# A mixture-of-experts kernel: weights loaded and split in 1024-column pieces, VectorE's lower halves a call behind

## The chip, the cores and the metric

The kernel runs on one core of one Trainium2 chip. The metric is the time of one execution in device microseconds; the text compares medians of several runs. TensorE (PE in the rows) multiplies, VectorE (DVE), ScalarE (ACT) and GpSimd (POOL) do the elementwise work, and SyncE (SP) issues most of the DMAs.

## What is computed

```python
def reference(...):
    # 1: gated linear attention, 4 x 8 heads, 768 steps, head size 48
    state = alpha[t][:, None] * state + outer(k[t], v[t]);  y[t] = q[t] @ state
    x = y, reshaped to 3072 rows of 384
    # 2: first mixture: rows whose skip score is over 0 go to one of 8 experts (384 -> 1024 -> 384)
    e = argmax(x @ w_gate);  x += gate * (relu(x @ w1[e]) @ w2[e])
    # 3: second mixture: all rows, the same sizes, weights of its own, without the residual
    e = argmax(x @ w_gate2); out = gate * (relu(x @ w1b[e]) @ w2b[e])
```

Inputs and outputs are float32. An expert's products are done in three 16-bit matmuls: each operand is split into an upper half (float16) and a lower half (the rest), and upper x upper, upper x lower and lower x upper are summed.

## The kernel before

The kernel has three stages. Attention runs over 24 groups of 128 steps (g = 0 to 23); for each group VectorE makes two scans (`pp`, L546, and `qka`, L550), GpSimd or VectorE multiply them into k and q (L554, L555), TensorE forms the products (`ap`, `kp`, `yp`, `sp`, `rp`), ScalarE evicts, and one of the two masks is on GpSimd (`at`, L572) and the other on VectorE (L574). The first mixture runs over nine rounds (j = 0 to 8) of up to 256 rows, rounds 0 and 1 with the same expert; the second mixture has nine rounds of up to 480 rows. In a round `ffn1` makes the hidden layer in pairs of 128 columns (first mixture): TensorE writes `hp`, ScalarE evicts the upper half `hh`, VectorE the lower half `hl`. `ffn2t` then makes `yp`, evicted as `yth` and `ytl`. Beside that, a generator `gate_rows` of the round before works out on VectorE where each row goes next: among its steps are `own`, `mv` and `hot` (the one-hot tile, L372), which TensorE multiplies into an index, `idx_ps` (L377). From the index GpSimd issues indirect DMAs that gather the rows (`xg`).

The order of the instructions is written out by hand: `tick`, `tick2` and the like are called after each piece of matmul work, and step the generators (`rt`, `release`) and the weight work (`background`) by tables of numbers.

Weights: `load_w(x, m)` loads matrix m (0 for w1, 384 x 1024, and 1 for w2, 1024 x 384) of expert x, 16 experts counting both mixtures, in one DMA on SyncE's queue into a float32 tile `raw` of 3072 columns; there are two such places. `queue_split` puts four pieces of 768 columns on a list, and each call of `background` takes one: ScalarE copies it to the upper half (`w0h` for w1, `w1h` for w2, L202), and VectorE or GpSimd subtract to give the lower half (`w0l`, `w1l`, L207). `ON_POOL` names the pieces whose subtraction is GpSimd's: 0 and 2 of expert 0, 1 to 3 of experts 1 to 8, none after that. The first GpSimd piece behind a VectorE piece is one column wider, so that it waits for it.

In attention `background` is called at even g from 6 on; in rounds 2 to 8 of the first mixture at f = 1, 3, 5, 7 of `ffn1` and four times in `ffn2t`.

Of the kernel before, what the change touches and what calls it, by code (L numbers as in the profile page):

```python
# [8 lines left out]
F32 = mybir.dt.float32  # L9
# [3 lines left out]
AF = mybir.ActivationFunctionType  # L13
ALU = mybir.AluOpType
# [59 lines left out]
ON_POOL = [(0, 2)] + [(1, 2, 3)] * 8 + [()] * 7  # L74
# [34 lines left out]
def body(tc, qka, vN, rw, wg2, wg17, w1a, w2a, w1b, w2b, cst, zr, out):  # L109
    nc = tc.nc  # L110
    V, A, P, T, SY = nc.vector, nc.scalar, nc.gpsimd, nc.tensor, nc.sync
    ctx = ExitStack()
    with ctx:
# [20 lines left out]

        with ExitStack() as fctx, tc.manual_schedule():
            wsp = fctx.enter_context(tc.tile_pool(name="wsp", bufs=2))
            wraw = fctx.enter_context(tc.tile_pool(name="wraw", bufs=2))
            em = fctx.enter_context(tc.tile_pool(name="em", bufs=1))
            ps = fctx.enter_context(tc.tile_pool(name="ps", bufs=1, space=PSUM))

# [3 lines left out]
            def bank(tag, name, *shape, parts=128):  # L144

                pool, bufs = phase.get(tag, (ps, 1))
                t = pool.tile([128, 512], F32, tag=tag, name=name, bufs=bufs)
                v = t[0:parts, 0:int(np.prod(shape))]
                if len(shape) == 2:
                    v = v.rearrange("p (a b) -> p a b", a=shape[0])  # L150
                elif len(shape) == 3:
                    v = v.rearrange("p (a b c) -> p a b c", a=shape[0], b=shape[1])
                return v
# [28 lines left out]
            raw = {}  # L182
            wt = {}
            regs = {}

            def load_w(x, m):
                if x >= 2 * E:
                    return
                src = ((w1a, w2a), (w1b, w2b))[x // E][m]
                src = src[bass.ds(regs[x], 1)].rearrange("o k f -> (o k) f") if x % E else src[0]  # L190
                t = wraw.tile([128, 3072], F32, tag="raw", name=f"raw{x}_{m}")
                kc = 3 if m == 0 else 8
                SY.dma_start(t.rearrange("p (k f) -> p k f", k=kc), src.rearrange("(k p) f -> p k f", p=128))
                raw[x, m] = t

            def split_w(x, m, s):
                if s == 0:
                    wt[x, m] = [wsp.tile([128, 3072], d, tag=f"w{m}{h}", name=f"w{m}{h}_{x}") for h, d in (("h", F16), ("l", BF16))]
                hi, lo = wt[x, m]
                r = raw[x, m]  # L200
                sl = slice(s * 768, (s + 1) * 768)
                A.activation(out=hi[:, sl], in_=r[:, sl], func=AF.Copy)  # L202
                eng = P if s in ON_POOL[x] else V
                if x and s and eng is P and s - 1 not in ON_POOL[x]:

                    sl = slice(s * 768 - 1, (s + 1) * 768)
                eng.tensor_tensor(lo[:, sl], r[:, sl], hi[:, sl], op=ALU.subtract)  # L207

            bg = []

            def queue_split(x, m):
                if x < 2 * E:
                    for s in range(4):
                        bg.append((x, m, s))

            def background(n=1):
                for _ in range(n):
                    if bg:
                        split_w(*bg.pop(0))

# [169 lines left out]
            def order(i, counts):  # L392
# [27 lines left out]
                for s in range(1, 8):  # L420
                    regs[8 * i + s] = nc.values_load(
                        perm[:, i, s:s + 1], engines=[mybir.EngineType.SP], min_val=0, max_val=7,
                        skip_runtime_bounds_check_because="places of a permutation of the experts")
                load_w(8 * i + 1, 0)
                yield 0
                cap = cc("caps")[:, 8 * i:8 * i + 8].rearrange("p (s o) -> p s o", o=1).to_broadcast([128, 8, 8])
# [26 lines left out]

            def ffn1(x, n, nf, xs, hs, each):

                (xh, xl), (hh, hl) = xs, hs
                wh, wl = [w.rearrange("p (k f) -> p k f", k=3) for w in wt[x, 0]]
                for f0 in range(0, 8, nf):
                    hp = bank("B", "hp", nf, n)
                    for i in range(nf):  # L460
                        f = slice((f0 + i) * 128, (f0 + i + 1) * 128)
                        for k in range(3):
                            T.matmul(hp[:, i], lhsT=wh[:, k, f], rhs=xh[:, k, 0:n], start=(k == 0), stop=False)  # L463
                            T.matmul(hp[:, i], lhsT=wh[:, k, f], rhs=xl[:, k, 0:n], start=False, stop=False)  # L464
                            T.matmul(hp[:, i], lhsT=wl[:, k, f], rhs=xh[:, k, 0:n], start=False, stop=(k == 2))  # L465
                        if i < nf - 1:
                            each(f0 + i)
                    A.activation(out=hh[:, f0:f0 + nf, 0:n], in_=hp, func=AF.Relu)  # L468
                    V.scalar_tensor_tensor(out=hl[:, f0:f0 + nf, 0:n], in0=hp, scalar=0.0, in1=hh[:, f0:f0 + nf, 0:n], op0=ALU.max, op1=ALU.subtract)  # L469
                    each(f0 + nf - 1)  # L470

            def ffn2(x, yp, hs, c, each):

                wh, wl = [w.rearrange("p (f d) -> p f d", f=8) for w in wt[x, 1]]
                for f in range(8):
                    T.matmul(yp, lhsT=hs[0][:, f, c], rhs=wh[:, f], start=(f == 0), stop=False)
                    T.matmul(yp, lhsT=hs[0][:, f, c], rhs=wl[:, f], start=False, stop=False)
                    T.matmul(yp, lhsT=hs[1][:, f, c], rhs=wh[:, f], start=False, stop=(f == 7))
                    each(f)

            def ffn2t(x, c0, c1, hs, yps, each):

                wh, wl = [w.rearrange("p (f d) -> p f d", f=8) for w in wt[x, 1]]
                for d, yp in enumerate(yps):
                    ds = slice(d * 128, (d + 1) * 128)
                    for f in range(8):
                        T.matmul(yp, lhsT=wh[:, f, ds], rhs=hs[0][:, f, c0:c1], start=(f == 0), stop=False)  # L487
                        T.matmul(yp, lhsT=wh[:, f, ds], rhs=hs[1][:, f, c0:c1], start=False, stop=False)  # L488
                        T.matmul(yp, lhsT=wl[:, f, ds], rhs=hs[0][:, f, c0:c1], start=False, stop=(f == 7))  # L489
                        each(d, f)  # L490
# [252 lines left out]
            emit_a(0)  # L743
            prep(2, halves)
            queue_split(0, 0)
            queue_split(0, 1)
            routes, orders = [], []
            for g in range(NB):
# [5 lines left out]
                if g > 0:  # L754
                    emit_r(g - 1)
                    i, k, n, _ = gof[g - 1]
# [30 lines left out]
                if g in (3, 6):  # L787
                    load_w(0, g // 6)
# [132 lines left out]
            for j in range(NJ):  # L921
                x = POS[j]
# [4 lines left out]
                if j != 1:  # L927
                    queue_split(x + 1, 0)
# [71 lines left out]
            for j in range(NJ):  # L1000
                x = E + POS[j]
# [84 lines left out]
                if j == 0:  # L1086

                    tot = bank("M", "tot", 18)
                    for c, src in ((0, cum[:, len(GROUPS), 0:8]), (8, cum2[:, NJ, :]), (16, cum[:, SPLIT, 0:1]), (17, cum2[:, NJ - LAST, 0:1])):
                        w = src.shape[-1]  # L1090
# [139 lines left out]
```

## Time and profile before

| | us |
|---|---|
| median of 3 runs | 529.93 (529.77 to 530.51) |
| the profiled execution | 529.54 |
| its span in the trace | 527.70 |
| TensorE busy | 491.6 (93%) |
| VectorE busy | 363.2 (69%) |
| GpSimd busy | 274.7 (52%) |
| ScalarE busy | 270.2 (51%) |

The times in the rows are microseconds from the start of the span. A row of the timeline gives start, duration, engine, line, operation and what is written from what, how many such instructions are merged, and in brackets how long the engine had been idle before and what ended that. TensorE's busy time is a share of the span by modelled ends of its matmuls; where it waits, a bracket says so.

### The profile page before, as it was taken

How to read it: one execution, taken by the hardware profiler on the slowest of the kernel's cores; microseconds unless marked ns; L12 is line 12 of the kernel's file. 1: busy time of each engine (PE TensorE's matmuls, PEld its weight loads, DVE VectorE, ACT ScalarE, POOL GpSimd, SP SyncE). 2: the span in 40 equal slices, each digit the busy share in tenths (PEclk: the TensorE clock that was granted, in tenths of full speed). 3: DMA queues.
4: the chain of work that ended last, by engine and by line, in shares of the span. 5: the costliest groups of instructions: out<-in, count | busy, mean ns of one | idle time of the engine just before them, and what ended most of it. 6: DMA issues, size and time to landing. Idle time of an engine off the chain costs nothing.

```text
span 527.7 us, 12035 instructions
## 1 busy us (share of the span) xinstructions
PE 491.6 (93%) x4701; PEld 378.5 (72%) x4701; DVE 363.2 (69%) x927; ACT 270.2 (51%) x545; POOL 274.7 (52%) x226
## 2 busy tenths in 40 slices
PE   5899998999986999998989899999999999999992
PEld 3788887878885999898979566565555666666662
DVE  7989997989697677888778845845537373737320
ACT  1545555465543666656656244734556464646320
POOL 2479978698426867687866153227024151311121
PEclk9999999999999999999999999999999999999997
DMA  8889784771285657767774076583535445450010
GB/s 282 324 293 324 221 278 152 254 226 48 64 255 185 204 172 259 254 202 267 223 260 145 25 252 245 161 281 89 176 111 188 149 154 169 139 186 29 17 39 27
DMA packets 44868, 96.74 MB, mean 183 GB/s; under 512 B 7049, under 2 KB 31879, under 8 KB 44806
## 3 DMA queue, kind: packets, MB, share of 16 engines
q1 hardware_dynamic: 36614, 77.68, 44.5%
q0 software_dynamic: 4736, 13.51, 7.6%
q10 hardware_dynamic: 3456, 4.72, 2.5%
q8 instruction: 39, 0.64, 0.5%
q14 instruction: 23, 0.19, 0.1%
HBM read 83.41 MB, written 12.99 MB: 183 GB/s over the span
## 4 chain that ended last, share of the span: by engine, by line
PE 59%; DVE 23%; issue 6%; POOL 5%; DMA 4%; ACT 1%; POOLq 0%; ACTq 0%; DVEq 0%
PE hp L463 8%; PE hp L465 8%; PE hp L464 8%; PE ypc L487 4%; PE ypc L489 4%; PE ypc L488 4%; DVE pp L546 4%; DVE qka L550 4%; PE tp L450 3%; PE yp L488 2%; PE yp L489 2%; PE yp L487 2%; DMA xg<-xrows,ixb 2%; PE rp L645 2%; DMA raw<-in_w1a 2%
## 5 line engine op out<-in xcount | busy, mean ns | idle before, releaser
L982 POOL DMA_INDIRECT out<-o,ixo x31 | 31.4, 1011 | 142.0 <-ACT o L1055 127.2
L469 DVE SCALAR_TENSOR_TENSOR h2l<-hp,h2h 128x352 f16<-128x352 f32 (+8 forms) x66 | 38.6, 585 | 64.1 <-ACT h2h L468 63.1
L463 PE MATMUL hp<-x2h,w0h 128*128 128x352 f16 (+8 forms) x216 | 68.7, 323 | 0.0
L465 PE MATMUL hp<-x2h,w0l 128*128 128x352 f16 (+8 forms) x216 | 68.7, 323 | 0.0
L464 PE MATMUL hp<-x2l,w0h 128*128 128x352 f16 (+8 forms) x216 | 68.7, 323 | 0.0
L468 ACT ACTIVATE h2h<-hp 128x352 f16<-128x352 f32 (+8 forms) x66 | 33.8, 513 | 46.6 <-PE hp L465 46.5
L207 POOL TENSOR_TENSOR w1l<-raw,w1h 128x768 bf16<-128x768 f32 (+1 forms) x26 | 43.0, 1681 | 27.0 <-ACT w1h L202 16.6
L463 PE MATMUL hp<-xh,w0h 128*128 128x200 f16 (+7 forms) x216 | 52.4, 252 | 4.8 <-DVE hl L469 3.9
L202 ACT ACTIVATE w0h<-raw 128x768 f16<-128x768 f32 x64 | 53.4, 836 | 4.5 <-ACT xy L646 1.7
L464 PEld LDWEIGHTS <-w0h 128*128 128x128 f16 x432 | 42.3, 98 | 18.5 <-issue 5.2
L441 POOL DMA_INDIRECT xg<-xrows,ix x41 | 49.2, 1200 | 11.6 <-issue 9.3
L488 PE MATMUL yp<-hl,w1h 128*128 128x200 f16 (+7 forms) x216 | 53.4, 255 | 0.5 <-DVE hl L469 0.4
L202 ACT ACTIVATE w1h<-raw 128x768 f16<-128x768 f32 x64 | 51.5, 836 | 4.3 <-DMA raw<-in_w2a 2.2
L487 PE MATMUL yp<-hh,w1h 128*128 128x200 f16 (+7 forms) x216 | 53.5, 255 | 0.0
L489 PE MATMUL yp<-hh,w1l 128*128 128x200 f16 (+7 forms) x216 | 53.5, 255 | 0.0
L465 PEld LDWEIGHTS <-w0l 128*128 128x128 bf16 x432 | 42.3, 98 | 15.2 <-issue 0.4
L464 PE MATMUL hp<-xl,w0h 128*128 128x200 f16 (+7 forms) x216 | 52.3, 252 | 0.1
L465 PE MATMUL hp<-xh,w0l 128*128 128x200 f16 (+7 forms) x216 | 52.4, 252 | 0.0
L463 PEld LDWEIGHTS <-w0h 128*128 128x128 f16 x432 | 42.3, 98 | 13.6 <-issue 0.5
L207 DVE TENSOR_TENSOR w0l<-raw,w0h 128x768 bf16<-128x768 f32 x38 | 39.7, 1046 | 13.0 <-ACT w0h L202 10.9
L207 POOL TENSOR_TENSOR w0l<-raw,w0h 128x768 bf16<-128x768 f32 (+1 forms) x26 | 44.1, 1720 | 4.7 <-ACT w0h L202 2.4
L554 POOL TENSOR_TENSOR qka<-qka 128x512 f32<-128x512 f32 (+1 forms) x24 | 28.5, 1186 | 29.8 <-DVE qka L550 22.9
(183 smaller groups left out, 1350.5 us busy)
## 6 DMA issues: line engine op xcount, KB each, us to landing
qka<-in_qka SPq DMA_DIRECT2D x21, 772.0 KB, 6.9
raw<-in_w1a SPq DMA_DIRECT2D x8, 1536.0 KB, 6.8
raw<-in_w2a SPq DMA_DIRECT2D x8, 1536.0 KB, 8.9
raw<-in_w1b SPq DMA_DIRECT2D x8, 1536.0 KB, 7.3
raw<-in_w2b SPq DMA_DIRECT2D x8, 1536.0 KB, 7.1
v<-in_vN SPq DMA_DIRECT2D x24, 192.0 KB, 3.5
xrows<-xy ACTq DMA_DIRECT2D x24, 192.0 KB, 4.4
xrows<-x SPq DMA_DIRECT2D x9, 197.0 KB, 4.8
```

The source lines that it names most:

```text
L202: A.activation(out=hi[:, sl], in_=r[:, sl], func=AF.Copy)
L207: eng.tensor_tensor(lo[:, sl], r[:, sl], hi[:, sl], op=ALU.subtract)
L441: P.indirect_dma_start(out=dst, out_offset=None, in_=xrows[0:rows], in_offset=bass.IndirectOffsetOnAxis(ap=ix, axis=0), bounds_check=rows ...
L463: T.matmul(hp[:, i], lhsT=wh[:, k, f], rhs=xh[:, k, 0:n], start=(k == 0), stop=False)
L464: T.matmul(hp[:, i], lhsT=wh[:, k, f], rhs=xl[:, k, 0:n], start=False, stop=False)
L465: T.matmul(hp[:, i], lhsT=wl[:, k, f], rhs=xh[:, k, 0:n], start=False, stop=(k == 2))
L468: A.activation(out=hh[:, f0:f0 + nf, 0:n], in_=hp, func=AF.Relu)
L469: V.scalar_tensor_tensor(out=hl[:, f0:f0 + nf, 0:n], in0=hp, scalar=0.0, in1=hh[:, f0:f0 + nf, 0:n], op0=ALU.max, op1=ALU.subtract)
L487: T.matmul(yp, lhsT=wh[:, f, ds], rhs=hs[0][:, f, c0:c1], start=(f == 0), stop=False)
L488: T.matmul(yp, lhsT=wh[:, f, ds], rhs=hs[1][:, f, c0:c1], start=False, stop=False)
L489: T.matmul(yp, lhsT=wl[:, f, ds], rhs=hs[0][:, f, c0:c1], start=False, stop=(f == 7))
L982: ins = P.indirect_dma_start(out=out, out_offset=bass.IndirectOffsetOnAxis(ap=ix, axis=0), in_=src, in_offset=None, bounds_check=N - 1, oo ...
```

## The change

There are six places of 1024 columns in place of two of 3072, the same memory. A w1 matrix is loaded and split in three pieces of 1024 columns, a w2 matrix in four of 768; each piece has a DMA and a place of its own, and a piece's load waits only for the piece six before it. ScalarE's upper half is issued by the call of `background` that takes the piece. If the lower half is VectorE's, it goes on a list `lows` and is issued by the next call, before that call's own piece; if it is GpSimd's, it is issued at once. The one column by which GpSimd's first piece was wider becomes an instruction of its own, since it lies in another place. `split_done` makes sure that a matrix is complete before its matmuls.

```diff
-            wraw = fctx.enter_context(tc.tile_pool(name="wraw", bufs=2))
+            wraw = fctx.enter_context(tc.tile_pool(name="wraw", bufs=6))
...
+            PIECES = ([(i * 1024, (i + 1) * 1024) for i in range(3)], [(i * 768, (i + 1) * 768) for i in range(4)])
             def load_w(x, m):
...
-                t = wraw.tile([128, 3072], F32, tag="raw", name=f"raw{x}_{m}")
-                kc = 3 if m == 0 else 8
-                SY.dma_start(t.rearrange("p (k f) -> p k f", k=kc), src.rearrange("(k p) f -> p k f", p=128))
-                raw[x, m] = t
+                src = src.rearrange("(k p) f -> p k f", p=128)
+                w = src.shape[2]
+                for s, (a, b) in enumerate(PIECES[m]):
+                    t = raw[x, m, s] = wraw.tile([128, 1024], F32, tag="raw", name=f"raw{x}_{m}{s}")
+                    SY.dma_start(t[:, 0:b - a].rearrange("p (k f) -> p k f", f=w), src[:, a // w:b // w, :])
+            lows = []
             def split_w(x, m, s):
...
-                A.activation(out=hi[:, sl], in_=r[:, sl], func=AF.Copy)
-                eng = P if s in ON_POOL[x] else V
-                if x and s and eng is P and s - 1 not in ON_POOL[x]:
-
-                    sl = slice(s * 768 - 1, (s + 1) * 768)
-                eng.tensor_tensor(lo[:, sl], r[:, sl], hi[:, sl], op=ALU.subtract)
+                A.activation(out=hi[:, a:b], in_=r[:, 0:b - a], func=AF.Copy)
+                if s not in ON_POOL[x]:
+                    lows.append((x, m, s))
+                    return
+                if x and s and s - 1 not in ON_POOL[x]:
+
+                    a0, b0 = PIECES[m][s - 1]
+                    P.tensor_tensor(lo[:, b0 - 1:b0], raw[x, m, s - 1][:, b0 - a0 - 1:b0 - a0], hi[:, b0 - 1:b0], op=ALU.subtract)
+                P.tensor_tensor(lo[:, a:b], r[:, 0:b - a], hi[:, a:b], op=ALU.subtract)
+            def flush():
+                for x, m, s in lows:
+                    hi, lo = wt[x, m]
+                    a, b = PIECES[m][s]
+                    V.tensor_tensor(lo[:, a:b], raw[x, m, s][:, 0:b - a], hi[:, a:b], op=ALU.subtract)
+                lows.clear()
...
             def background(n=1):
                 for _ in range(n):
+                    flush()
                     if bg:
                         split_w(*bg.pop(0))
+            def split_done(x, m):
+
+                while any(b[0:2] == (x, m) for b in bg):
+                    background()
+                if any(b[0:2] == (x, m) for b in lows):
+                    flush()
```

VectorE's queue at the start of round 4, before (names as above; a number behind a name is its buffer, and line numbers are each program's own):

```order
L353 TENSOR_REDUCE own<-ge 128x2
L469 SCALAR_TENSOR_TENSOR hl<-hp,hh 128x2x232
L207 TENSOR_TENSOR w0l_3262<-raw_0_3091,w0h_3261 128x768
L356 TENSOR_TENSOR own<-cs,own 128x16
L469 SCALAR_TENSOR_TENSOR hl<-hp,hh 128x2x232
L360 SCALAR_TENSOR_TENSOR own<-own,r 128x2
L365 TENSOR_TENSOR mv<-on,own 128x128
```

The same place of VectorE's queue in the changed program:

```order
L378 TENSOR_REDUCE own<-ge 128x2
L495 SCALAR_TENSOR_TENSOR hl<-hp,hh 128x2x232
L381 TENSOR_TENSOR own<-cs,own 128x16
L495 SCALAR_TENSOR_TENSOR hl<-hp,hh 128x2x232
L223 TENSOR_TENSOR w0l_3310<-raw_00_3128,w0h_3309 128x1024
L385 SCALAR_TENSOR_TENSOR own<-own,r 128x2
L390 TENSOR_TENSOR mv<-on,own 128x128
```

The lower half w0l moves behind the second pair's hl and is 1024 columns wide.

VectorE's queue at the end of round 0, where the index read (ixr, ixb) releases a gather, before:

```order
L939 TENSOR_SCALAR gs<-xg 128x2
L940 TENSOR_SCALAR gs<-xg 128x2
L207 TENSOR_TENSOR w0l_2317<-raw_0_2073,w0h_2316 128x768
L387 COPY ixr<-idx_ps 128x48
L388 SCALAR_TENSOR_TENSOR own<-idx_ps,ixr 128x48
L702 CAST ixb<-own 128x1
```

The same place in the changed program, down to where w0l now stands:

```order
L967 TENSOR_SCALAR gs<-xg 128x2
L968 TENSOR_SCALAR gs<-xg 128x2
L412 COPY ixr<-idx_ps 128x48
L413 SCALAR_TENSOR_TENSOR own<-idx_ps,ixr 128x48
L730 CAST ixb<-own 128x1
L732 TENSOR_TENSOR own<-idx_94,own 128x48
L459 TENSOR_TENSOR pr<-place_95,own 128x98
L462 TENSOR_REDUCE own<-pr 128x14
L463 CAST ix_114<-own 128x14
L735 COPY idx_94<-own 128x32
L976 TENSOR_TENSOR ytl_2194<-yp,yth_2193 128x200
L223 TENSOR_TENSOR w0l_2335<-raw_00_2081,w0h_2334 128x1024
```

The lower half goes from ahead of the index read to behind the first ytl.

GpSimd's queue in attention, from its second lower half of w1 (w0l, at g = 10) on, before:

```order
L207 TENSOR_TENSOR w0l_706<-raw_0_504,w0h_705 128x768
L572 AFFINE_SELECT at<-at 128x512
L554 TENSOR_TENSOR qka<-qka 128x512
L555 TENSOR_TENSOR qka<-qka,pp 128x512
L572 AFFINE_SELECT at<-at 128x512
L554 TENSOR_TENSOR qka<-qka 128x512
L555 TENSOR_TENSOR qka<-qka,pp 128x512
L572 AFFINE_SELECT at<-at 128x512
```

The same stretch of the changed program's queue, from its second w0l on:

```order
L217 TENSOR_TENSOR w0l_716<-raw_02_508,w0h_715 128x1024
L600 AFFINE_SELECT at<-at 128x512
L582 TENSOR_TENSOR qka<-qka 128x512
L583 TENSOR_TENSOR qka<-qka,pp 128x512
L600 AFFINE_SELECT at<-at 128x512
L582 TENSOR_TENSOR qka<-qka 128x512
L583 TENSOR_TENSOR qka<-qka,pp 128x512
L217 TENSOR_TENSOR w1l_1198<-raw_10_707,w1h_1197 128x768
L600 AFFINE_SELECT at<-at 128x512
```

The first w2 piece (w1l) of expert 0 comes on GpSimd 6 rows of `qka` and `at` work behind that w0l; before it came after 12, two groups later. The third w2 piece moves by two groups as well.

## Rows read from the trace of the kernel before

**Rows 1.** Busy time by stage: stretch, length, engines (instructions), TensorE's granted clock, DMA share, GB/s.
```profile
146.00:174.00 28.00, 22.26 (x323) 21.31 (x323) 22.18 (x86) 11.56 (x26) 13.94 (x16) 0.94 0.66 215
...
170.00:171.00 1.00, 1.00 (x12) 0.94 (x11) 0.93 (x8) 0.31 (x2) 0.00 (x0) 0.50 1.02 420
...
174.00:291.00 117.00, 110.56 (x1183) 105.72 (x1180) 92.64 (x316) 73.13 (x130) 86.05 (x63) 1.00 0.67 221
...
318.00:508.00 190.00, 190.00 (x1174) 114.85 (x1173) 100.83 (x192) 99.34 (x175) 54.50 (x49) 1.00 0.43 144
```

**Rows 2.** TensorE's longest wait: us in total, times, longest.
```profile
PE idx_ps L377 <- DVE hot L372: 7.1, 5, 2.6
```

**Rows 3.** Timeline of round 4, several engines.
```profile
206.31 4.85 POOL L207 TENSOR_TENSOR w1l<-raw,w1h 128x769 bf16<-128x769 f32 x3 [3.79 <-DVE w1l L207]
...
210.42 1.55 DVE L207 TENSOR_TENSOR w0l<-raw,w0h 128x768 bf16<-128x768 f32 x1
...
210.88 0.56 ACT L468 ACTIVATE hh<-hp 128x464 f16<-128x464 f32 x1 [0.50 <-PE hp L465]
...
212.52 0.15 DVE L360 SCALAR_TENSOR_TENSOR own<-own,r 128x2 f32<-128x2 f32 x1
...
216.01 0.23 PE L377 MATMUL idx_ps<-mv,hot 128*128 128x64 f16 x2 [0.92 <-DVE hot L372]
```

**Rows 4.** Timeline of rounds 6, 7 and 8, several engines.
```profile
239.66 4.86 POOL L207 TENSOR_TENSOR w1l<-raw,w1h 128x769 bf16<-128x769 f32 x3 [3.96 <-DVE w1l L207]
...
256.90 0.13 POOL L942 MEMSET x<- 128x16 f32 x1
256.98 4.85 POOL L207 TENSOR_TENSOR w1l<-raw,w1h 128x769 bf16<-128x769 f32 x3
...
260.57 0.84 ACT L202 ACTIVATE w0h<-raw 128x768 f16<-128x768 f32 x1 [1.54 <-DMA raw<-in_w1a]
...
266.60 0.23 PE L377 MATMUL idx_ps<-mv,hot 128*128 128x64 f16 x2 [2.64 <-DVE hot L372]
...
283.33 0.25 PE L488 MATMUL yp<-hl,w1h 128*128 128x200 f16 x1 [0.36 <-DVE hl L469]
```

**Rows 5.** Timeline of rounds 0 and 1, several engines.
```profile
155.57 0.95 DVE L207 TENSOR_TENSOR w0l<-raw,w0h 128x768 bf16<-128x768 f32 x1
...
161.00 4.83 POOL L207 TENSOR_TENSOR w0l<-raw,w0h 128x769 bf16<-128x769 f32 x3
...
161.70 0.26 PE L450 MATMUL tp<-cs,xg 80*128 80x80 f32 x1 [1.43 <-DMA xg<-xrows,ixb]
...
162.87 3.01 DVE L969 COPY cum<-cum 128x8 f16<-128x8 f16 x1
...
168.03 0.20 PE L463 MATMUL hp<-xh,w0h 128*128 128x80 f16 x1 [2.97 <-DVE hl L469]
```

**Rows 6.** Timeline of attention, several engines.
```profile
49.33 0.44 SPq L531 DMA_DIRECT2D qka<-in_qka  x1
...
55.15 2.58 POOL L207 TENSOR_TENSOR w0l<-raw,w0h 128x768 bf16<-128x768 f32 x1
...
77.56 2.58 POOL L207 TENSOR_TENSOR w0l<-raw,w0h 128x768 bf16<-128x768 f32 x1
...
81.72 0.31 PE L606 MATMUL yp<-at,v 128*48 128x128 f32 x1 [1.61 <-POOL at L572]
...
86.14 1.29 DVE L207 TENSOR_TENSOR w0l<-raw,w0h 128x768 bf16<-128x768 f32 x1 [0.33 <-ACT w0h L202]
...
114.22 1.19 POOL L554 TENSOR_TENSOR qka<-qka 128x512 f32<-128x512 f32 x1 [1.18 <-DVE qka L550]
...
117.53 0.38 PE L566 MATMUL ap<-qka 64*128 64x128 f32 x2 [1.10 <-POOL qka L555]
```

**Rows 7.** DMA issues: what, queue, times, KB each, median us from issue to landing.
```profile
raw<-in_w1a SPq DMA_DIRECT2D x8, 1536.0 KB, 6.8
...
v<-in_vN SPq DMA_DIRECT2D x24, 192.0 KB, 3.5
```

More of the change, by code (lines that the diff above doesn't have):

```diff
@@ L199, in split_w @@
                 hi, lo = wt[x, m]
-                r = raw[x, m]
-                sl = slice(s * 768, (s + 1) * 768)
-                A.activation(out=hi[:, sl], in_=r[:, sl], func=AF.Copy)
-                eng = P if s in ON_POOL[x] else V
-                if x and s and eng is P and s - 1 not in ON_POOL[x]:
-                    sl = slice(s * 768 - 1, (s + 1) * 768)
-                eng.tensor_tensor(lo[:, sl], r[:, sl], hi[:, sl], op=ALU.subtract)
+                r = raw[x, m, s]
+                a, b = PIECES[m][s]
[10 more added lines that the diff above has]
+                    hi, lo = wt[x, m]
+                    a, b = PIECES[m][s]
+                    V.tensor_tensor(lo[:, a:b], raw[x, m, s][:, 0:b - a], hi[:, a:b], op=ALU.subtract)
+                lows.clear()
             bg = []
@@ L212, in queue_split @@
                 if x < 2 * E:
-                    for s in range(4):
+                    for s in range(len(PIECES[m])):
                         bg.append((x, m, s))
@@ L454, in ffn1 @@
             def ffn1(x, n, nf, xs, hs, each):
+                split_done(x, 0)
                 (xh, xl), (hh, hl) = xs, hs
@@ L472, in ffn2 @@
             def ffn2(x, yp, hs, c, each):
+                split_done(x, 1)
                 wh, wl = [w.rearrange("p (f d) -> p f d", f=8) for w in wt[x, 1]]
@@ L481, in ffn2t @@
             def ffn2t(x, c0, c1, hs, yps, each):
+                split_done(x, 1)
                 wh, wl = [w.rearrange("p (f d) -> p f d", f=8) for w in wt[x, 1]]
```

## The prediction, made before the changed kernel was run

> **What bounds the kernel now.** I read the busy time and granted clock by stage first, then who TensorE waits for, then the order of time around each of those waits. By stage [rows 1], TensorE is busy for all 190 us of the second mixture's steady part (318 to 508), 110.56 of 117 us in rounds 2 to 8 of the first mixture (174 to 291) and 22.26 of 28 us in rounds 0 and 1. So a weight load or split that moves in the second mixture costs nothing as long as the weights are ready, and what the change is worth is read from the idle TensorE time of attention and of the first mixture. The list of TensorE's waits has one large entry, the index matmul for VectorE's one-hot tile "hot": 7.1 us in five places [rows 2]. Four of these are in rounds 4 to 7, once a round, such as 0.92 us at 216.01 [rows 3] and 2.64 us at 266.60 [rows 4]. The others are in rounds 0 and 1 [rows 5] and in attention [rows 6].
>
> **What sets those waits.** In rounds 4 to 7 VectorE works without a pause from the first pair's lower half to "hot". One row on the way is too long: w0l takes 1.55 us from 210.42 [rows 3], where the same instruction takes 0.95 at 155.57 [rows 5]. GpSimd's three w1l pieces end at 206.31 + 4.85 = 211.16, and w0l ends 0.81 later, at 211.97 [rows 3]. VectorE was held until GpSimd's run ended. Round 7 looks like a late load, as ScalarE waits 1.54 us for raw, but GpSimd's w1l run ends only at 256.98 + 4.85 = 261.83 [rows 4], so w0l, which follows that ScalarE piece, would have been held anyway. The copy of cum at 162.87 tells more: it arrives in the second of three w0l pieces on GpSimd and ends at 165.88, right after the third (161.00 + 4.83 = 165.83) [rows 5]. GpSimd does not let VectorE in between pieces queued back to back.
>
> The Trainium skill ("SBUF — State Buffer", section "SBUF: two separate sides") says that VectorE with two SBUF inputs, or in a fast mode, and GpSimd lock each other out of a shared port for a whole instruction. By that rule alone the copy would have got in after the second piece, 1.6 us earlier; the measured row decides. With the rule, round 6 below would gain 0.2 us and rounds 0 and 1 would give less, and the sum would be about +1.6 instead of +1.45.
>
> **The change part by part.** A w1 piece grows by a third in width, so by at most a third in time: VectorE's 0.95 becomes at most 1.27 (I take 1.2, as a part of it is fixed), GpSimd's 1.62 (a third of 4.85) at most 2.16. A w2 piece keeps its width. The one-column GpSimd instruction is not in the trace; it lies between GpSimd's memset of 16 columns, 0.13 us [rows 4], and 1.62; I take 0.2, by the memset.
>
> *Rounds 4 and 5.* The flush puts w0l behind the second pair's lower half hl. Before, w0l filled the time in which VectorE waits for that pair: hl could only start when ScalarE's hh of 210.88 ended, near 211.44 [rows 3]. Afterwards VectorE idles until 211.44, hl runs for 0.55 (211.97 to 212.52 before, from w0l's end to the next row), w0l for 1.2, and the next instruction (own, L360) starts near 213.2 instead of 212.52 [rows 3]. Everything from there to "hot" is the same chain, so the wait at 216.01 grows by 0.65. Round 5 has the same pattern: +1.3 for both. GpSimd's run starts later too, since VectorE's w1l now stands behind a ytl (some 0.7 us), ends near 212.0 and just misses holding w0l.
>
> *Round 6.* GpSimd's run ends at 239.66 + 4.86 = 244.52 [rows 4], plus up to 0.9 for the later w1l and the one-column piece. w0l, by the pattern of round 4 ready at about that time, is free or held 0.5 us: +0.1 to +0.55; I take +0.3.
>
> *Round 7.* ScalarE's late load goes away, as the first piece needs only its own place. w0l is still held to 261.83 or a little later, so the 2.64 us at 266.60 stay: 0 (from -1.1, if GpSimd's run started sooner, to +0.3).
>
> *Round 8.* w0l moves from before the second hl to between the two x instructions, and the exponential that ScalarE must do before the last hh gets its input later, by an estimate 0.4 to 0.5 us (w0l's 1.2 are now on the way to it, less the 0.7 to 0.8 by which w0l delayed the second hl before, where the pattern of round 4 holds); TensorE's 0.36 us at 283.33 [rows 4] grow by that: +0.45. Rounds 2 and 3 have no such wait: 0. First mixture from round 2: +2.05.
>
> *Rounds 0 and 1.* w0l at 155.57 stood ahead of the index read that releases the gather; taking it away moves the gather about 0.9 us earlier (nearly the length of that row), and TensorE's 1.43 us at 161.70 shrink to 0.6. But TensorE then waits at 168.03 (2.97 us) for VectorE, which is held by GpSimd until 165.83 [rows 5]. That end moves by the gather's 0.4 to 0.9 (w0l now contends with the gathers' issue) and by the shorter run, 0.2 + 2 x 2.16 = 4.5 instead of 4.83: -0.7 to -1.2, I take -0.9.
>
> *Attention.* Eight pieces become seven, and GpSimd's stand elsewhere. The piece at 77.56 grows from 2.58 to between 3.05 and 3.44, straight onto TensorE's 1.61 us at 81.72: +0.5 to +0.9. VectorE's piece at 86.14 (1.29 us) goes, which gives about 1 back on VectorE's chain. GpSimd gets a piece two groups earlier than the one it had, ahead of the mask before 114.22, where it had 1.18 us idle: 1.65 to 2.58 more, less that idle time and less the lead, against the 1.10 us at 117.53 [rows 6]. Bounds: -1.1 (that wait goes) to +1.7 (both waits grow); I take +0.3. The fourth w2 piece needs the first place, so SyncE waits for GpSimd's first lower half, about 58.5 with a third more than 55.15 + 2.58, and one v and one qka load, before at 49.33, stand behind it [rows 6]. That qka tile is loaded three groups before VectorE's scan reads it; with that cover I take nothing, and if it were gone the scan, and with it GpSimd's qka, would wait for what is missing, a microsecond at most.
>
> *Second mixture, loads.* 80 more DMAs on SyncE (2 for each of 16 w1, 3 for each of 16 w2), none on a path that TensorE waits for: 0.
>
> **Sum.** 2.05 - 0.9 + 0.3 = +1.45 us on the profiled execution of 529.54 (span 527.7 and 1.84 around it): 530.99. The median of the runs shown is 0.39 above that execution: **531.4**. About 0.2% (1.06 us) is what a measurement of this kernel can tell from no change.
>
> **Rivals.** *Faster: the clock dip goes.* After the waits of 1.43 and 2.97 us within 8 us the granted clock is 0.50 at 170, the lower of the two levels, 1.2 GHz; over 146 to 174 it is 0.94, so 0.06 x 28 = 1.7 us are lost [rows 1]. After 2.64 us at 266.60 it did not fall (1.00 in 174 to 291). Afterwards 0.6 and some 2.9 us remain: between the two. If the dip goes and attention's wait at 117.53 goes with it: 1.45 - 1.7 - 1.4 = -1.65, 528.3. Chance 0.18.
>
> *No change.* w0l at its plain 0.95 x 1.2 fits better than I think in rounds 4 and 5 (GpSimd's run, not the idle time, decides), or round 7 loses a microsecond: the terms cancel, 530.1. Chance 0.26. It speaks for it that the gains and losses are each about a microsecond.
>
> *Slower by more.* GpSimd is the late engine of attention: both waits grow and the held qka load is late as well, +1.7 instead of +0.3, and round 6 takes 0.55: 533.1. Chance 0.13.
>
> *Small loads arrive late.* A 192 KB load lands in 3.5 us where 1536 KB take 6.8 [rows 7]: small loads pay for themselves in latency. If three pieces did not overlap (3 x 4.5 = 13.5 instead of 6.8), the last piece of w1 would come after its turn, and ScalarE would hold hh by up to 2 us in six rounds: +12, 543. SyncE issues them back to back, so they overlap: 0.03. The Trainium skill ("DMA: Bandwidth & Descriptors", section "Bandwidth") asks for DMAs of at least 1 MiB and speaks against the 384 and 512 KB pieces; no row here shows such a piece alone.
>
> The forecast itself, 530.4 to 532.6, has 0.40.
>
> **How the numbers follow.** Slower by over 0.2% (above 531.0): 0.36 of the forecast, 0.13 and 0.03, so 0.52; within 0.2%: 0.04 and 0.25, so 0.29; faster: 0.18 and 0.01, 0.19. The range is 528.4 to 533.6: the faster rival's middle to just above the slower one's, leaving some 0.2 outside.
>
> **What would show it.** Right: VectorE's w0l in rounds 4 and 5 near 1.2 us and not held, idle time before the second hl, and index waits of about 1.5 us; the gather of round 0 issued 0.9 us after the gs rows sooner than before; no wait of ScalarE for raw in round 7, with the index wait there still over 2 us. Wrong: a clock of 1.00 through 168 to 173, an index wait in round 7 under 1.5 us, waits of VectorE's scan for qka in the second third of attention, or idle TensorE time in the second mixture.

## The result and the profile of the changed kernel

| | before | changed |
|---|---|---|
| median (17 runs each, side by side) | 530.51 us | 536.59 us |
| lowest and highest | 529.67 to 534.91 | 531.63 to 541.80 |
| the profiled execution | 529.54 | 534.40 |
| its span | 527.70 | 532.70 |

The ratio is 1.0067, with an interval of 1.0039 to 1.0096; the four executions of the changed kernel above 541 us, those with the lowest mean granted clock (0.969), are left out of it. The kernel is slower, as forecast, but by about 3.6 us by the ratio and 6.1 by the medians, where 1.45 were forecast, and the median lies above the range. One number needs explaining before the others: the executions of the changed kernel lie 10 us apart, and their mean granted clock goes with that in the main, from 0.987 down to 0.969.

The busy time by stage of the changed kernel (columns as in [rows 1]; the column behind the engines is TensorE's granted clock):

```profile
146.00:174.00 28.00, 22.50 (x307) 21.66 (x307) 23.51 (x87) 11.88 (x26) 15.30 (x17) 0.88 0.69 209
171.00:172.00 1.00, 1.00 (x19) 1.00 (x18) 0.87 (x2) 0.83 (x3) 0.30 (x2) 0.50 0.03 11
174.00:291.00 117.00, 107.52 (x1151) 103.06 (x1148) 91.14 (x294) 67.68 (x117) 79.51 (x67) 0.99 0.72 221
252.00:256.00 4.00, 4.00 (x29) 3.53 (x26) 3.38 (x14) 0.57 (x2) 3.69 (x3) 0.57 0.79 221
318.00:508.00 190.00, 190.00 (x1196) 116.06 (x1194) 100.44 (x188) 100.09 (x171) 51.76 (x49) 1.00 0.48 151
```

The second mixture is as full as before. In rounds 2 to 8 TensorE is busy for 3 us less of the same 117. The clock is low for longer in rounds 0 and 1 (0.88 instead of 0.94 over the 28 us), and it falls a second time, at 252 to 256, where the kernel before had 1.00.

TensorE's long waits, of the changed kernel (us in total, times, longest; the first answers to [rows 2]):

```profile
PE idx_ps L402 <- DVE hot L397: 9.5, 5, 3.1
PE hp L489 <- DVE hl L495: 4.8, 2, 3.9
```

Rounds 4, 6 and 7 of the changed kernel in the timeline (start, duration; they answer to [rows 3, 4]):

```profile
211.40 0.56 ACT L494 ACTIVATE hh<-hp 128x464 f16<-128x464 f32 x1 [0.28 <-PE hp L491]
211.99 0.64 DVE L495 SCALAR_TENSOR_TENSOR hl<-hp,hh 128x464 f16<-128x464 f32 x1 [1.06 <-ACT hh L494]
212.55 1.22 DVE L223 TENSOR_TENSOR w0l<-raw,w0h 128x1024 bf16<-128x1024 f32 x1
213.68 0.16 DVE L385 SCALAR_TENSOR_TENSOR own<-own,r 128x2 f32<-128x2 f32 x1
...
217.18 0.23 PE L402 MATMUL idx_ps<-mv,hot 128*128 128x64 f16 x2 [1.57 <-DVE hot L397]
...
246.76 1.65 DVE L223 TENSOR_TENSOR w0l<-raw,w0h 128x1024 bf16<-128x1024 f32 x1
...
251.80 0.23 PE L402 MATMUL idx_ps<-mv,hot 128*128 128x64 f16 x2 [2.16 <-DVE hot L397]
...
261.89 4.85 POOL L217 TENSOR_TENSOR w1l<-raw,w1h 128x768 bf16<-128x768 f32 x3
...
265.33 2.49 DVE L223 TENSOR_TENSOR w0l<-raw,w0h 128x1024 bf16<-128x1024 f32 x1
...
271.18 0.23 PE L402 MATMUL idx_ps<-mv,hot 128*128 128x64 f16 x2 [3.07 <-DVE hot L397]
```

In round 4 VectorE idles for 1.06 us, does hl, then w0l in 1.22 us, and own starts 2.28 us after ScalarE's hh started (1.64 before, [rows 3]). In rounds 6 and 7 w0l is longer than 1.22: it is held by GpSimd's run of w1l (to 261.89 + 4.85 = 266.74 in round 7; w0l ends at 267.82).

Where the 5.00 us of the profiled execution arise, by the start times of TensorE's instructions:

| stretch, to | before | changed | difference | forecast |
|---|---|---|---|---|
| first hidden matmul of round 0 | 146.12 | 146.50 | +0.38 | +0.3 |
| hidden matmul of round 1 behind the long wait | 21.91 | 21.39 | -0.52 | -0.9 |
| index matmul of round 4 | 47.98 | 49.29 | +1.31 | +0.65 |
| of round 5 | 16.55 | 17.30 | +0.75 | +0.65 |
| of round 6 | 16.74 | 17.32 | +0.58 | +0.3 |
| of round 7 | 17.30 | 19.38 | +2.08 | 0 |
| last index matmul (303.09, 308.49) | 36.49 | 37.31 | +0.82 | +0.45 |
| end | 224.61 | 224.21 | -0.40 | 0 |

The waits account for +0.65, +0.76, +0.57 and +0.43 of rounds 4 to 7. What is left, 0.66 ahead of round 4 and 1.65 ahead of round 7, goes with the clock: around round 1 it is at 0.50 for some 7 us (in part while TensorE waits) instead of some 3.5, and behind round 6 the 4 us at 0.57 cost 4 x 0.43 = 1.7 us.

### The profile page after: what moved, and what is told of

Read it like the earlier page. It is cut to its first block, busy times and chain, and to the rows that moved or that the text cites. A ratio compares the mean times of both kernels' runs of the same rounds, so it can differ in the third digit from the quotient of the medians.

```text
span 532.7 us, 12347 instructions
## 1 busy us (share of the span) xinstructions
PE 495.4 (93%) x4701; PEld 381.0 (72%) x4701; DVE 367.1 (69%) x919; ACT 267.6 (50%) x529; POOL 272.7 (51%) x234
## 4 chain that ended last, share of the span: by engine, by line
PE 59%; DVE 21%; POOL 9%; issue 7%; ACT 1%; DMA 1%; POOLq 0%; SPq 0%; DVEq 0%; ACTq 0%
PE hp L491 8%; PE hp L489 7%; PE hp L490 7%; PE ypc L515 4%; PE ypc L517 4%; PE ypc L516 4%; DVE qka L578 3%; DVE pp L574 3%; PE tp L475 3%; POOL qka L583 3%; PE yp L516 2%; PE yp L515 2%; PE yp L517 2%; PE yp L503 2%; PE yp L505 2%
## 5 line engine op out<-in xcount | busy, mean ns | idle before, releaser
L515 PE MATMUL yp<-hh,w1h 128*128 128x200 f16 (+7 forms) x216 | 54.6, 260 | 0.4 <-ACT hh L494 0.4
L516 PE MATMUL yp<-hl,w1h 128*128 128x200 f16 (+7 forms) x216 | 54.6, 260 | 0.4 <-DVE hl L495 0.4
L209 ACT ACTIVATE w0h<-raw 128x1024 f16<-128x1024 f32 x48 | 50.2, 1049 | 1.2 <-ACT xy L674 1.2
L217 POOL TENSOR_TENSOR w1l<-raw,w1h 128x768 bf16<-128x768 f32 x26 | 43.9, 1716 | 0.0
L517 PEld LDWEIGHTS <-w1l 128*128 128x128 bf16 x336 | 33.9, 101 | 10.5 <-POOL w0l L217 0.5
L515 PE MATMUL ypc<-h2h,w1h 128*128 128x440 f16 (+4 forms) x120 | 40.6, 338 | 0.0
```

Of the source, the lines that this page charges most:

```text
L209: A.activation(out=hi[:, a:b], in_=r[:, 0:b - a], func=AF.Copy)
L217: P.tensor_tensor(lo[:, a:b], r[:, 0:b - a], hi[:, a:b], op=ALU.subtract)
```

## The experiments

The theory was that the late place of VectorE's lower halves makes the waits longer, and that the longer waits make the clock fall, in more executions and places than before. The rivals were the wider pieces, the split loads, and a clock that falls whatever the kernel does. The medians below stand beside runs of the kernel before on the same chip (530.7 to 531.2 us); "at once" is behind ScalarE's copy, as before.

**e1: the changed kernel with all lower halves at once.**

```diff
                     lows.append((x, m, s))
+                    flush()
                     return
```

> The changed kernel with one difference: VectorE's lower halves are issued at once, behind ScalarE's copy, and not a call later. If the place behind the second hl makes the loss: the index waits of rounds 4 to 7 fall from 1.57, 1.65, 2.16 and 3.07 us to at most 1.2, 1.2, 1.9 and 2.9, the granted clock is 1.00 from 240 to 291 us, and the time is 529.5 to 531.5 us (within 0.3% of the kernel before). If the wider pieces or the smaller loads make it: the waits of rounds 4 and 5 stay above 1.4 us and the time stays above 533 us.

Measured: 536.42 us, ratio 1.0085 (1.0053 to 1.0116). Index waits 1.42, 1.07, 1.41 and 2.55. The waits moved roughly as the theory of the place says, but not in round 4: there w0l, wide and at once, takes 1.83 us, since GpSimd's run holds it, and the wait is nearly that of the late place. The time did not move: attention now ends at 154.53 instead of 146.50. Three things were in that: two falls of the clock in attention (at 18 to 25 and 86 to 90 us), a late start in this one execution (TensorE waits 1.71 us at 17.43), and slower attention, which e3 separates.

**e2: the kernel before (768 columns, whole loads) with the lower halves a call late.** The same list and `flush`, put into `split_w` and `background` of the kernel before.

> The kernel before (768 columns, two places, whole loads) with VectorE's lower halves a call later. If the place makes the loss: the second hl runs first (to 211.44 + 0.55), then w0l with 0.95, so own starts at 212.94 instead of 212.52 and the waits of rounds 4 and 5 grow from 0.9 to 1.3 to 1.5 us; those of rounds 6 and 7 to 1.6 to 2.0 and 2.6 to 3.0; the clock falls in some executions and the time is 530.5 to 534 us. If wider pieces or smaller loads make it: waits as before, 529.7 to 530.5 us.

Measured: 535.43 us, 1.0077 (1.0047 to 1.0107). Index waits 1.42, 1.57, 2.37 and 2.96: in the ranges given for rounds 4 and 7, a little above for 5, 0.4 above for 6. The median is 1.4 us above the time expected. In rounds 4 and 5 the place alone, without wide pieces or split loads, makes these waits. In rounds 6 and 7 it makes them in another way than the changed kernel: w0l takes its plain 0.95 us, held by nothing, but the second hl is late. In round 6 ScalarE waits 1.32 us for raw (at 246.26), as a piece that is read late keeps the place of its whole matrix; in round 7 it waits 1.78 us ahead of the same piece (there the row names GpSimd's w1l). The clock falls at 268 to 276 besides 168 to 172.

**e3: the changed kernel, late only for the first piece of w1 of experts 2 to 8.**

```diff
                     lows.append((x, m, s))
+                    if not (m == 0 and 2 <= x <= 8):
+                        flush()
                     return
```

> The changed kernel, but only the first piece of w1 of experts 2 to 8 is still a call late (rounds 2 to 8); all other lower halves of VectorE at once. If that one piece carries the loss: index waits as in the changed kernel (1.57, 1.65, 2.16, 3.07, each within 0.2), the two long waits of rounds 0 and 1 as before (1.4 and 3.0), time 532 to 537 us. If the loss comes from the other late pieces (attention, rounds 0 and 1, the w2 pieces): time 529.5 to 531.5 us with index waits below 1.2 in rounds 4 and 5.

Measured: 536.57 us, 1.0102 (1.0070 to 1.0134). Index waits 1.58, 1.65, 1.72 and 1.80: rounds 4 and 5 as expected, 6 and 7 far below the changed kernel's. Round 7 of e3 and the end of its attention, in the timeline:

```profile
261.81 4.86 POOL L219 TENSOR_TENSOR w1l<-raw,w1h 128x768 bf16<-128x768 f32 x3 [0.21 <-ACT w1h L209]
267.27 1.22 DVE L225 TENSOR_TENSOR w0l<-raw,w0h 128x1024 bf16<-128x1024 f32 x1
271.86 0.23 PE L404 MATMUL idx_ps<-mv,hot 128*128 128x64 f16 x2 [1.80 <-DVE hot L399]
```

```profile
82.90 0.31 PE L636 MATMUL yp<-at,v 128*48 128x128 f32 x1 [2.08 <-POOL at L602]
118.00 0.31 PE L636 MATMUL yp<-at,v 128*48 128x128 f32 x1 [1.58 <-POOL at L602]
150.81 0.25 PE L491 MATMUL hp<-xh,w0h 128*128 128x200 f16 x1 [0.87 <-DVE lg L678]
```

In round 7 GpSimd's run ends at 266.67, before w0l starts, and w0l takes its plain 1.22. So the loss in rounds 4 and 5 is w0l's own late place; in rounds 6 and 7 of the changed kernel it is mostly VectorE's w1l (0.44 and 1.27 us of the waits), which also comes a call late and starts GpSimd's run later against TensorE's work. Attention ends at 150.81, 4.3 us later than in the changed kernel, with no fall of the clock between 20 us and there: wide pieces at once cost more there than late ones. From 24 to 150 us TensorE's waits for `at` are 1.15 us longer than in the changed kernel and those for VectorE's `lg` 1.8 us; where the rest arises was not traced.

**e6: the changed kernel, late only for expert 0 (in attention).**

```diff
                     lows.append((x, m, s))
+                    if x:
+                        flush()
                     return
```

> The changed kernel with VectorE's lower halves a call late only for expert 0 (attention), and at once for all others. If the late place costs in the rounds and the wide pieces at once cost in attention (e1 and e3: attention ends at 150.8 us instead of 146.5): attention ends at 146.5, the index waits are those of e1 (1.42, 1.07, 1.41, 2.55), the span is about 528.6 and the time 530 to 532 us. If the loss of e1 and e3 in attention is not the place: attention ends at 149 us or later and the time stays above 533.

Measured: 532.34 us, 1.0033 (1.0005 to 1.0060), index waits 1.42, 1.06, 1.40 and 2.55, attention to 147.99 with the clock down to 0.75 and 0.82 at 80 to 88. The waits are as expected, and so is attention but for that fall (4 x 0.25 + 4 x 0.18 = 1.7 us, so 146.3 without it), which came behind a wait of only 1.62 us at 81.82; the median is 0.3 us above the range given. Attention wants the late place with wide pieces, the rounds don't.

**e5: the kernel before with its loads split, nothing else** (eight places of 768 columns; each piece of w1 that crosses a row of 1024 has two loads, and GpSimd's extra column an instruction of its own).

```diff
-            wraw = fctx.enter_context(tc.tile_pool(name="wraw", bufs=2))
+            wraw = fctx.enter_context(tc.tile_pool(name="wraw", bufs=8))
...
+                for s in range(4):
+                    t = raw[x, m, s] = wraw.tile([128, 768], F32, tag="raw", name=f"raw{x}_{m}{s}")
```

> The kernel before with nothing but its loads split: eight places of 768 columns, each piece with loads of its own, the same pieces on the same engines, all at once. If the loads are neutral: the index waits of rounds 4 to 6 stay at 0.9, 0.9 and 1.6 us, attention ends (first hidden matmul of round 0) within 0.4 us of 146.1, and the time is within 0.2% of the kernel before. If the small loads or the loads of v and qka that wait behind them on SyncE's queue make the loss: waits for raw, v or qka appear in attention or in rounds 3 to 7, and the time is over 0.5% above.

Measured: 532.05 us, 1.0036 (1.0012 to 1.0060). Between the two expectations: attention ends at 146.09, no wait for raw, v or qka appears among TensorE's, and ScalarE's waits for raw in the rounds are gone; but the index waits are 0.97, 1.06, 1.75 and 2.89, each 0.05 to 0.25 longer, the wait of round 1 is 3.68, and the clock falls at 268 to 276 too. The loads themselves are not late; why the waits grow by these tenths was not separated (GpSimd's extra instruction of 0.2 us is a candidate).

The waits by width and place, from e5, e1, e2 and the changed kernel (sum of the four index waits, end of attention without further falls of the clock where there is such an execution):

| | at once | a call late |
|---|---|---|
| four pieces of 768 | 6.67 / 146.09 | 8.32 / 147.30 |
| 1024 for w1 | 6.45 / 150.81 | 8.45 / 146.50 |

The narrow late case (e2) has whole loads, and what ScalarE's waits in rounds 6 and 7 cost is in its 8.32. With wide pieces the late place adds 2.0 us to the waits of the rounds. The width, at once, adds nothing to their sum (0.45 more in round 4, 0.34 less in each of rounds 6 and 7); in attention place and width depend on each other.

**e4 and e7: matmuls that nothing reads, in TensorE's waits of the changed kernel.** They write a free part of PSUM and nothing waits for them.

```diff
+                fill(FILL.get(i - len(GROUPS), 0))
                 for k in range(n):
                     T.matmul(idx_ps[...], lhsT=hot[:, k, :], rhs=mv[:, k], ...)
...
                     hp = bank("B", "hp", nf, n)
+                    if n == 80 and f0 == 6:
+                        fill(14)
```

> The changed kernel with matmuls that nothing reads put into TensorE's waits: 14 of 432 columns ahead of the fourth pair of round 1, 6, 6, 8 and 12 ahead of the index matmuls of rounds 4 to 7. If the idle time of TensorE makes the clock fall: the instructions behind the waits start at the same time as in the changed kernel within 0.3 us until 167, the clock is 1.00 from 160 to 291 us, the time is 530 to 532 us and its runs lie within 2 us of each other. If the clock falls for another reason (the chip's state, not the waits): two falls as before, 533 to 541 us. If the fill itself delays the work: waits gone but the time above that of the changed kernel.

Measured: 533.00 us, 1.0041 (1.0010 to 1.0073), 10 of 12 runs within 2 us. The table of e4 was one round off: round 4 had none and the 12 stood in round 8, where TensorE did not wait, so they cost about 2.2 us there. e7 puts them right.

> The changed kernel with the unread matmuls of e4 in the right rounds (6, 6, 8 and 12 ahead of the index matmuls of rounds 4 to 7, 14 in round 1). If idle time makes the clock fall and the 12 misplaced matmuls of e4 cost it 12 x 0.18 us: span 529 us, clock 1.00 from 20 to 520 us, time 530 to 531.8 us, runs within 2 us of each other but for one or two. If the clock falls whatever TensorE does: 533 to 541 us.

Measured: 530.85 us (530.02 to 532.63), 1.0015 (1.0001 to 1.0028). Round 4 and the stages of e7:

```profile
214.17 1.26 PE L349 MATMUL fl<-rg 128*128 128x432 f16 x6
215.90 0.23 PE L411 MATMUL idx_ps<-mv,hot 128*128 128x64 f16 x2 [0.48 <-DVE hot L405]
```

```profile
166.00:174.00 8.00, 6.01 (x110) 5.11 (x109) 7.30 (x37) 4.05 (x11) 4.37 (x6) 1.00 0.56 186
174.00:291.00 117.00, 113.94 (x1196) 106.98 (x1195) 93.02 (x304) 70.36 (x120) 79.75 (x67) 1.00 0.73 221
```

No dependence between the other instructions has changed, yet the median falls by 5.7 us, the runs draw together from 10 us to 2.6, and in the profiled execution the clock is 1.00 from 20 to 508 us. So it was TensorE's idle time that made the clock fall. How much of the loss that is shows only beside e8, since the same matmuls make the kernel before faster too.

**e8 and e9: the same matmuls in the kernel before** (11 in round 1, then 3, 3, 6 and 11; e9 has 9 more in attention, in TensorE's wait at 12 us).

> The kernel before with unread matmuls in its waits: 11 in round 1 and 3, 3, 6 and 11 ahead of the index matmuls of rounds 4 to 7. If the fall of the clock at 169 to 173 us is worth what it takes from TensorE (1.7 us): clock 1.00 there, time 527.7 to 528.7 us, 0.2 to 0.5% below the kernel before. If VectorE's chain ends last there and hides it: within 0.2% of the kernel before.

Measured: 527.99 us, 0.9964 (0.9943 to 0.9985). With the waits filled in both, the two kernels are 530.85 - 527.99 = 2.9 us apart by the medians, where they were 6.1 apart; so the clock made 3.2 us of the 6.1. By the ratios 3.6 us become 2.7 (1.0015 against 0.9964), and the clock's share is only 0.9; what it made of the loss lies between these two. Seven runs of e8 lie at 527.3 to 528.3, five at 530.4 to 531.1. The profiled execution is of the second kind; its clock at the start of attention, and behind the filled waits:

```profile
16.00:20.00 4.00, 2.99 (x32) 2.56 (x29) 3.93 (x7) 1.87 (x7) 1.69 (x2) 0.50 1.04 374
20.00:24.00 4.00, 4.00 (x28) 3.34 (x28) 3.75 (x11) 1.20 (x2) 2.60 (x3) 0.50 0.40 161
...
166.00:174.00 8.00, 6.64 (x125) 5.40 (x124) 7.39 (x25) 2.46 (x9) 5.12 (x5) 1.00 0.50 171
174.00:291.00 117.00, 114.38 (x1233) 108.21 (x1230) 92.55 (x321) 74.03 (x132) 85.27 (x63) 1.00 0.67 223
```

> The kernel before with the unread matmuls of e8 and 9 more of 512 columns ahead of the scores of the second group in attention, where TensorE waits 2.5 us at 12 us. If the fall of the clock between 12 and 24 us (one length in most executions of e8, twice that in its profile) is on TensorE's path: clock 1.00 from 10 to 30 us, time 525.3 to 526.8 us, and the runs at 530.4 to 531.1 us of e8 are gone. If attention's start is set by VectorE: 527.3 us as e8, with its second group of runs.

Measured: 528.28 us (527.68 to 529.02), 0.9950 (0.9932 to 0.9968). The second group of runs is gone, but the low end is no lower: the first fall of the clock only moved, and a wait took its place (the timeline of e9):

```profile
18.72 1.91 PE L581 MATMUL ap<-qka 64*128 64x128 f32 x16 [3.03 <-DVE at L589]
```

VectorE's mask sets the start there; the time expected was missed by 1.5 us. e8 and e9 are faster than both kernels.

**e10 and e11: w0l out of VectorE's way to "hot".** Four calls late instead of one: behind hot and sh, just ahead of w1l. e10 on the kernel before, e11 with split loads (ten places of 768); both with unread matmuls.

```diff
+                if eng is V and m == 0 and 2 <= x <= 8:
+                    lows.append([4, lo[:, sl], r[:, sl], hi[:, sl]])
+                    return
```

> As e9 (fills 0, 0, 3 and 7 ahead of the index matmuls of rounds 4 to 7, as the waits get shorter), and VectorE's first lower half of w1 of experts 2 to 8 four calls of background later, behind hot and sh and just ahead of its w1l. If w0l on VectorE's way to hot is what TensorE waits for: idle TensorE time ahead of the index matmul below 0.3 us in rounds 4 and 5, by 0.9 to 1.5 us shorter in rounds 6 and 7, and 2.5 to 3.5 us less than e9. If something else on that way ends last: the waits stay within 0.3 us and the time is e9's. If the place in raw, which it holds some 10 us longer, makes the next load late: waits of ScalarE for raw of over 1 us in rounds 4 to 7 and no gain.

Measured: 545.20 us, 1.0266 (1.0234 to 1.0297): the third case. The piece read late holds the place of the whole matrix; ScalarE waits for the load, with hh queued behind it (round 5 of e10):

```profile
231.67 0.84 ACT L202 ACTIVATE w0h<-raw 128x768 f16<-128x768 f32 x1 [4.04 <-DMA raw<-in_w1a]
...
237.00 0.29 PE L399 MATMUL idx_ps<-mv,hot 128*128 128x64 f16 x2 [4.11 <-DVE hot L393]
```

Its clock also fell three times in the rounds, at 237, 257 and 278 us, for some 1.7 us each.

> As e10, but with the loads of e5 (four pieces of 768 columns, ten places instead of eight), so that the piece that is read late holds its own place only; unread matmuls as in e10. If e10 was slow by the late load of the whole matrix (ScalarE waited up to 4.0 us for raw and held hh behind it) and w0l on VectorE's way to hot is what TensorE waits for: no wait for raw over 0.3 us, own (the first of the two instructions behind the second hl) some 0.55 us earlier in rounds 4 and 5, idle TensorE time ahead of the index matmuls at most 0.5, 0.6, 1.0 and 2.0 us with the unread matmuls' time added (0.97, 1.06, 1.75 and 2.89 in e5), time 525 to 527 us. If something else than w0l sets hot: waits as in e5, time 528 to 529.5 us. If VectorE's w0l just ahead of w1l makes GpSimd's run late and holds mv: waits of over 2 us in rounds 4 and 5.

Measured: 529.14 us, 0.9965 (0.9947 to 0.9983). Rounds 5 and 6 of e11:

```profile
233.77 0.23 PE L407 MATMUL idx_ps<-mv,hot 128*128 128x64 f16 x2 [0.51 <-DVE hot L401]
...
242.76 0.25 PE L497 MATMUL hp<-xl,w0h 128*128 128x216 f16 x1 [1.13 <-DVE xl L482]
```

The index waits are 0.44 and 0.51 in rounds 4 and 5 and gone in 6 and 7, in the bounds given: w0l does set "hot". But the time expected, 525 to 527, was missed. w0l and w1l now stand ahead of VectorE's xl, for which TensorE waits 1.13 and 1.51 us two matmuls into rounds 6 and 7, and in the profiled execution TensorE waits 3.00 us for the gather of round 1 (1.65 in e9). Its clock also falls twice where that of e9 does not, some 1.7 us each:

```profile
84.00:88.00 4.00, 4.00 (x29) 3.68 (x28) 1.48 (x5) 1.95 (x6) 4.00 (x5) 0.61 0.81 265
...
164.00:168.00 4.00, 3.24 (x48) 3.16 (x49) 2.38 (x5) 0.68 (x2) 3.84 (x4) 0.71 0.68 220
168.00:172.00 4.00, 4.00 (x57) 3.07 (x55) 3.04 (x14) 0.71 (x3) 1.75 (x3) 0.87 0.35 101
```

So this execution as a whole says little of the move, and even the fastest of the runs, 527.85, lies above the time expected. From the first hidden matmul of round 2 to the last index matmul, where neither has a fall, e11 takes 128.4 us against 129.5 in e9: 1.1 us gained of the 2.5 to 3.5 expected. Most of what the move freed came back as another wait; and it needs split places at all.

## Why the prediction was wrong

**The step that failed is the clock.** The prediction's sum has no term for the granted clock. It met the clock only in the rival "the clock dip goes", as a gain, and dismissed a further fall with one row: after 2.64 us at 266.60 it did not fall. That was one wait in one execution. In the profiled executions here it fell behind waits of 2.16 us (changed kernel, 251.80), 2.96 (e2), 2.89 (e5), 2.55 and even 1.62 (e6), and did not behind 3.07 (changed kernel, 271.18), 2.55 (e1) and 1.62 (e7). Every term that lengthened a wait should have carried a share of 1.7 us, the price of a fall that [rows 1] already gave. Worked out in the same way, four waits that grow to between 1.5 and 3 us put up to 4 x 1.7 = 6.8 us in play (an estimate), and the upper end of the range should have been near 540. No rival held this case. e7 and e8 show it: filling the idle time takes 5.7 us off the changed kernel and 2.8 off the kernel before, so of the 6.1 us between them 3.2 go with the clock (by the ratios 0.9 of 3.6). The other 2.9 alone would have given 530.51 + 2.9 = 533.4 us, inside the range.

**What the change costs without the clock** is e7 against e8, both filled. From the first hidden matmul of round 0 to the last index matmul it is 304.96 - 146.59 = 158.37 and 305.39 - 149.24 = 156.15: +2.2 us, where the prediction had 2.05 - 0.9 = +1.15. By the medians it is 530.85 - 527.99 = 2.9. So the sum of the waits was also 1 to 1.5 us too small, in these terms:

- *Rounds 4 and 5: right.* +0.65 and +0.76 against +0.65; hl runs first, VectorE idles ahead of it, w0l takes 1.22 (1.2 taken) and is not held. e2 shows that the place alone does it. In round 4 the early place would have cost about as much with a wide piece (1.42 in e1), as GpSimd's run holds it.
- *Rounds 6 and 7: mis-sized.* +0.57 and +0.43 where +0.3 and 0 were taken (bounds 0.55 and 0.3). Round 7's mechanism was right, as w0l is held by GpSimd's run and ScalarE's wait for raw is gone; but the later w1l, priced with the run's end alone, also moves that run against hl, and e3 gets 1.72 and 1.80 with w1l at once. The prediction saw the later w1l and did not ask what it does to round 7. Its "without a pause" does not hold for round 7 of the kernel before, where VectorE idles 1.79 us ahead of w0l at 261.45.
- *Round 8: right in its main term.* Two waits of 0.40 and 0.36 instead of one of 0.36, where +0.45 was taken; the rest of the +0.82 are short waits such as 0.28 us for ohm at 290.50.
- *Rounds 0 and 1: direction right, -0.5 for -0.9.* The gather comes 0.86 us sooner after the gs rows, as forecast (0.48 us from the start of the span, 156.87 for 157.35), and TensorE's wait for it is gone, not 0.6. But the term that failed is what this lead does to GpSimd's run, taken at 0.4 to 0.9: one gather's issue took 1.82 us beside w0l (1.00 before), and the run starts at 161.34 instead of 161.00. So its end hardly moves, 165.69 for 165.83, although the run is shorter as worked out (0.20 + 4.21 for 4.5 forecast). TensorE's second wait is 3.87 us for 2.97.
- *Attention: +0.38 for +0.3,* by other terms: the wait of 1.61 at 81.72 stayed (1.63), as GpSimd came to the longer piece (3.06 us) 0.49 us earlier, at 77.07; 0.88 us at 115.12 are new, and 1.10 at 117.53 became 0.62. The agreement is partly luck: e3 shows 4.3 us hanging on whether VectorE's wide pieces are late, which no term held. The rival of a late GpSimd in attention lies near that, but the changed kernel does not show it. Its rows (they answer to [rows 6]) are in the timeline:

```profile
81.72 0.31 PE L634 MATMUL yp<-at,v 128*48 128x128 f32 x1 [1.63 <-POOL at L600]
115.12 0.31 PE L634 MATMUL yp<-at,v 128*48 128x128 f32 x1 [0.88 <-POOL at L600]
118.34 1.16 PE L594 MATMUL ap<-qka 64*128 64x128 f32 x16 [0.62 <-POOL qka L583]
```

- *Split loads: no late load, as forecast;* still e5 is 0.36% slower, which the prediction had at nothing.

The gather's end in rounds 0 and 1 in the timeline of the changed kernel (it answers to [rows 5]):

```profile
161.48 4.21 POOL L217 TENSOR_TENSOR w0l<-raw,w0h 128x1024 bf16<-128x1024 f32 x2
161.66 4.06 DVE L997 COPY cum<-cum 128x8 f16<-128x8 f16 x1
...
167.89 0.23 PE L489 MATMUL hp<-xh,w0h 128*128 128x80 f16 x1 [3.87 <-DVE hl L495]
```

The copy of cum again ends (165.72) with GpSimd's run (165.69), over two pieces of 2.1 us. The Trainium skill ("SBUF — State Buffer", section "SBUF: two separate sides") gives the shared port to the engine that starts first for one whole instruction; by that the copy would have had its turn when the first piece ended, near 163.6. This trace differs, as the trace of before did: it waited for both.

Of the rivals, "small loads late" did not come (no wait for raw in e5), "no change" and "the clock dip goes" fell with the clock, and "slower by more" (533.1) has the direction but another cause. What the prediction named as signs of right came true, all of it: rounds 4, 5 and 7 and the gather of round 0. So these signs spoke for its waits and not for its time. Of what it named as wrong, "a clock of 1.00 through 168 to 173" points the other way: it stayed at 0.50 for longer.

Open: why VectorE's wide pieces at once cost attention 4 us, why split loads alone lengthen the waits by tenths, and what decides in one execution whether the clock falls behind a given wait.

## What to carry to other kernels

A wait on the path of TensorE has two prices, its length and a possible fall of the clock behind it; where several waits of a few microseconds stand in a row, forecast the fall as a case of its own, and look at the spread of the runs and their mean clock before believing one profile. Unread matmuls in the wait separate the two, and may be worth keeping. Whether a piece of side work should come at once or late depends on what the engine would otherwise wait for at that place: read it per stage, and include the piece that starts another engine's run.

## What was not expected of the hardware

- Behind waits of TensorE of 1.6 to 3.1 us the granted clock fell to 0.50, that is from 2.4 to 1.2 GHz, in some places and not in others of the same length; a fall costs about 1.7 us (4 us at 0.57). 46 unread matmuls of 432 columns (e7), and 34 (e8), kept it at 1.00 from 166 to 291 us in the profiled executions of both kernels.
- The kernel before loses by it too: filling its waits saves 2.8 us (530.82 and 527.99, medians side by side).
- VectorE's copy of 8 columns took 4.06 us: it ended only when two GpSimd instructions queued back to back had ended. In round 4 of the kernel before a gs row of 2 columns did the same, 1.97 us from 217.10, to the end of a run of three (214.19 + 4.85 = 219.04).
